# Decode attention kernel: the first weight load in two transfers, and TensorE's loop head at slot 128 of its instruction block

## The chip, the cores and the metric

One core of a Trainium2 chip runs the whole program. The metric is the device time of one execution in microseconds (us). Seven runs of the kernel before are shown, and beside them one execution that the hardware profiler recorded.

## What is computed

It is one decode step for 8 sequences: a sliding-window attention layer and then a small MLP, both behind a layer norm, in bf16. What matters of the reference:

```python
W = 2048                                   # max(256, Sk // 4), Sk = 8192
q = layernorm(x) @ wq                      # x: 8 x 512, wq: 512 x 4096, 32 heads of 128
k = repeat(k_cache[:, :, Sk - W:, :], 4)   # 8 sequences x 8 kv heads x 2048 x 128
v = repeat(v_cache[:, :, Sk - W:, :], 4)
p = softmax((q @ k^T) * 128 ** -0.5)
h = x + (p @ v).reshape(8, 4096) @ wo      # wo: 4096 x 512
y = layernorm(h)                           # then, for one token (the shifted branch is zero):
x1 = layernorm(y)
out = h + y + gelu(x1 @ w3) @ w4           # w3: 512 x 1792, w4: 1792 x 512
```

The program reads 79.18 MB from HBM: 67 MB of keys and values, 4 MB each of wq and wo, 1.8 MB each of w3 and w4.

## The kernel before, in words

**Transfers.** All large loads are issued by SyncE (SP) in `sp_prog`, on one DMA queue, in the order of the list `order`: first wq (L234, 4 MB), then keys of sequence 0 in two halves of four heads each (k, 2 MB each, L246), the first half of the last sequence's values (vl), the first quarter of wo (L252). Then, for b = 0 to 6: two key transfers of sequence b + 1 and two value transfers of sequence b, 2 MB each. At the end come the other half of the last values, the rest of wo, w3 (L258, two pieces) and w4 (L265, three pieces of 1 MB, 512 KB and 256 KB; the last has rows of 2 KB). Below, k0, k1, k2 and so on are the key transfers in order: k0 and k1 are sequence 0, k2 and k3 sequence 1. A key transfer from k2 on waits until the transposes of the keys two transfers earlier are done, since it overwrites their slot (L240: `sem_Thi`). A value transfer waits for the product that read its slot (L242). The first quarter of wo waits for the query product (L250), because it lies where wq lay. Each transfer of 128 rows is spread by rows over 16 DMA engines, eight rows for each engine.

**The query.** TensorE waits in `pe_q` for the transposed layer norm and for wq (L361), and then multiplies: 32 matmuls at L367 (`S_ps<-slots,xlnT`). The result is scaled, transposed back (L393) and put into `q_all` and `qcur`.

**The loop over sequences.** TensorE alone runs a hardware loop of 8 passes (`pe_main`, L591); the other engines' programs are unrolled. A pass (`pe_block`) transposes the keys (`pe_T`, L438, 8 steps of 16 matmuls), transposes the previous sequence's probabilities (`pe_P`, L454), sums them (`pe_LB`, L510), multiplies queries by keys (`pe_QK`, L478, 8 steps of 4) and, from the second pass on, multiplies the previous sequence's probabilities by its values (`pe_PV`, L535) and arranges the result (`pe_OP`, L554). The last two stand under an `If_ne` (L577) and are jumped over in the first pass, where there is no previous sequence. So the first pass waits for keys k0 at step 0 and for k1 at step 4, the second for k2 and k3.

**After the loop** (`pe_last` and what follows) come the last sequence's probabilities and values, the product with wo (L668, 128 matmuls), the norm's sums (L686), the product with w3 (L733, 56 matmuls) and that with w4 (L761, 56 matmuls, in three parts that each wait for their piece of w4). VectorE and ScalarE then write the two halves of the output, and SP stores it (L270).

**TensorE's instruction slots.** A matmul is two instructions, a weight load (PEld) and a matmul (PE); with fp32 operands it is two of each. A separate wait is one more. TensorE's code comes in blocks of 256 slots, and `head_slot` gives the slot of a block at which the loop's first instruction is put; what lies between is branched over. The program's own code ahead of the loop is 102 slots. A pass is 663: 384 up to and with the branch of the `If`, 276 for what it guards, 3 at the end. The code after the loop is 829 slots and follows directly.

Of the kernel before, what the change touches and what calls it, by code (L numbers as in the profile page):

```python
# [14 lines left out]
DH = 128  # L15
# [7 lines left out]
KC = D // 128  # L23
# [4 lines left out]
C = W // PP  # L28
# [8 lines left out]
def bass_sequential_preLN__sliding_block_cached__mixer_s_mlp__decode_kernel(  # L37
# [24 lines left out]
    with es:  # L62
        sb = lambda shape, dtype, name: es.enter_context(nc.sbuf_tensor(name, shape, dtype))
        ps_t = lambda shape, dtype, name: es.enter_context(nc.psum_tensor(name, shape, dtype))
        S = lambda name: es.enter_context(nc.semaphore(name))
# [3 lines left out]
        wq_sb = slots[:, NS - 2:NS, :].rearrange("p a e -> p (a e)")  # L69
# [71 lines left out]
        sem_v = [S(f"sem_v{i}") for i in range(2)]  # L141
        sem_vl = [S(f"sem_vl{i}") for i in range(2)]
        sem_x = S("sem_x")
        sem_wq = S("sem_wq")
        sem_w3 = [S(f"sem_w3_{i}") for i in range(2)]
        sem_w4 = [S(f"sem_w4_{i}") for i in range(3)]
        sem_wo = [S(f"sem_wo{i}") for i in range(3)]
# [83 lines left out]
        w4_sb = slots[:, place[("w4", 0)], 0:FC * D].rearrange("p (k n) -> p k n", k=FC)  # L231

        def sp_prog(e):
            e.dma_start(wq_sb, A_wq.rearrange("(p k) n -> p (k n)", k=KC)).then_inc(sem_wq, 16)  # L234

            for kind, t in order:
                if kind in ("k", "v", "vl"):
                    b, gq = divmod(t, 2) if kind != "vl" else (NB - 1, t)
                    if kind == "k" and b:
                        e.wait_ge(sem_Thi, NT * (t - 1))  # L240
                    if kind == "v" and b:
                        e.wait_ge(sem_PV[gq], b)  # L242
                    cache, sem, slot = {"k": (A_k_cache, sem_k, 0), "v": (A_v_cache, sem_v, 2),
                                        "vl": (A_v_cache, sem_vl, 4)}[kind]
                    src = cache[b, GL * gq:GL * (gq + 1), W0:SK, :].rearrange("g (p c) d -> p g (c d)", c=C)
                    e.dma_start(slots[:, slot + gq, :], src).then_inc(sem[gq], 16)  # L246
                    continue
                if kind == "wo":
                    if t == 0:
                        e.wait_ge(sem_peP, PEP_Q2)  # L250
                    f0, f1 = WO_CUT[t] * D, WO_CUT[t + 1] * D
                    e.dma_start(wo_sb[:, f0:f1], A_wo.rearrange("(p j) n -> p (j n)", j=NJ)[:, f0:f1]).then_inc(sem_wo[t], 16)  # L252
                    continue
                dst = slots[:, place[kind, t], :]
                if kind == "w3":
                    for i in range(2):
                        k0, k1 = i * KC // 2, (i + 1) * KC // 2
                        e.dma_start(w3_sb[:, k0:k1, :],  # L258
                                    B_w3.rearrange("(k p) f -> p k f", k=KC)[:, k0:k1, :]).then_inc(sem_w3[i], 16)
                else:  # L260
                    e.wait_ge(sem_Thi, NT * (NTILE - 1))
                    for i in range(len(W4_CUT) - 1):
                        c0, c1 = W4_CUT[i], W4_CUT[i + 1]
                        j = min(4, c1 - c0)
                        e.dma_start(w4_sb[:, c0:c1, :].rearrange("p (c j) n -> p c (j n)", j=j),  # L265
                                    B_w4[c0 * 128:c1 * 128, :].rearrange("(c p j) n -> p c (j n)", p=128, j=j)
                                    ).then_inc(sem_w4[i], 16)
            e.wait_ge(sem_dveP, DVEP_OUT_READY)
            e.wait_ge(sem_actP, ACTP_OUT_READY)
            e.dma_start(out.rearrange("b s d -> (b s) d"), out_sb[:, :]).then_inc(sem_out, 16)  # L270
            e.wait_ge(sem_out, 16)
# [86 lines left out]

        def pe_q(e):
            e.wait_ge(sem_dveP, DVEP_XLNT)  # L360
            e.wait_ge(sem_wq, 16)  # L361
            ins = None
            for k in range(2):
                for kc in range(KC):
                    for j in range(4):
                        n0 = (2 * j + k) * 512
                        ins = e.matmul(S_ps[32 * j:32 * j + B, k, :], xlnT[:, kc * B:(kc + 1) * B],  # L367
                                       wq_v[:, kc, n0:n0 + 512], start=(kc == 0), stop=(kc == KC - 1),
                                       tile_position=(0, 32 * j), skip_group_check=True)
                ins.then_inc(sem_peP, 1)  # L370
        PE.append(pe_q)

        ACTP_Q = ev_act.next()
# [187 lines left out]
        def pe_block(e, i, later=None):  # L561
            p = 2 * NT * i
            for t in range(NT):
                pe_T(e, i, t)
            pe_P(e, i, 0)
            pe_P(e, i, 1)
            pe_LB(e)
            pe_QK(e, p)
            pe_QK(e, p + 1)
            for t in range(NT, 2 * NT):  # L570
                pe_T(e, i, t)
                pe_QK(e, p + t - 2)
            pe_QK(e, p + 6)
            pe_QK(e, p + 7)
            if i == 0:
                return
            with nullcontext() if e is None else e.If_ne(later, 0):  # L577
                log.append("later")
                for gq in range(2):
                    need(e, sem_v[gq], 16 * i)  # L580
                    if e is not None:
                        pe_PV(e, 2 + gq, gq)
                pe_OP(e, i - 1)

        def pe_main(e):
            pe_block(None, 0)
            first = list(log)
            later_on = e.alloc_register("later_on")
            e.reg_mov(later_on, 0)
            log.clear()  # L590
            with nc.Fori(0, NB, engines=(mybir.EngineType.PE,), head_slot={mybir.EngineType.PE: 0}):  # L591
                pe_block(e, 1, later_on)
                e.reg_mov(later_on, 1)
            body = list(log)
            assert first == body[:body.index("later")]
            for i in range(2, NB):
                log.clear()
                pe_block(None, i)
                assert log == body, i
        PE.append(pe_main)  # L600

        for i in range(NB):
            p = 2 * NT * i
# [181 lines left out]
        with nc.Block() as block:  # L785
            block.gpsimd(pool_prog)
            block.sync(sp_prog)

            @block.tensor
            def _(e):  # L790
                for f in PE:
                    f(e)

            @block.scalar
            def _(e):
                for f in AC:
                    f(e)

            @block.vector
            def _(e):  # L800
                for f in DV:
                    f(e)
# [28 lines left out]
```

## Time and profile before

| | us |
|---|---|
| median of the 7 runs (lowest, highest) | 193.53 (193.14, 194.33) |
| the profiled execution: its time | 193.84 |
| its span, first to last instruction | 192.1 |
| TensorE (PE) busy | 145.8 |
| VectorE (DVE) busy | 85.9 |
| ScalarE (ACT) busy | 93.4 |
| wq: from its issue to its landing | 12.4 |

The profile's page gives busy times of the engines, the span cut in 40 slices with the granted TensorE clock (PEclk), the share of the DMA engines' time (DMA) and the rate (GB/s), the DMA queues, the chain of work that ended last, and the costliest groups of instructions. In the lists, "PE L668" is a TensorE matmul of line 668, "PEld" its weight load, "SPq" SyncE's sequencer. In square brackets stands how long the engine had been idle and what ended that; "issue" there means that no event in the profile ended it. Beside the lists the trace holds one record for each DMA packet (queue, start, length, bytes) and for each step of a transfer's semaphore, of which there are 16, one for each DMA engine. All times in the text are counted from the start of the span.

### The profile page before, as it was taken

Reading aid. Unit: us, or ns where it says so; the run is one execution under the profiler, and the core shown is the slowest. Engines: PE = TensorE matmul, PEld = TensorE weight load, DVE = VectorE, ACT = ScalarE, POOL = GpSimd, SP = SyncE. Lnnn points to the kernel's source line nnn. Section 1 sums busy time; section 2 is a strip of 40 time slices with the busy share of each in tenths; the row PEclk is TensorE's granted clock in tenths of the full one; section 3 lists DMA queues with packets and bytes.
Section 4 is the critical chain, followed back from the end, with each engine's and each line's share of the span. In section 5 each row is a group of like instructions: output and inputs, shape, how many; then the busy total and the mean of one; then the engine's idle time right before and its main releaser. Section 6 shows DMA issues by size and latency. Waiting matters only on the chain. (4 is left out here: it accounts for less than half of the span.)

```text
span 192.1 us, 6348 instructions
## 1 busy us (share of the span) xinstructions
PE 145.8 (76%) x2848; PEld 118.7 (62%) x2848; DVE 85.9 (45%) x183; ACT 93.4 (49%) x119; POOL 6.4 (3%) x17
## 2 busy tenths in 40 slices
PE   2038996399969964999599749997999599987654
PEld 0014964496757744876487539766976497676642
DVE  7922655155527450555174403643455245550031
ACT  3031744664476643744676436465745564552041
POOL 8400000000000000000000000000000000000000
PEclk9999999669999998799999985999799969999555
DMA  6999999999999999999999999999999999999991
GB/s 220 437 427 433 420 418 442 369 437 433 433 428 427 427 437 432 433 423 437 433 430 430 430 427 437 433 433 423 437 433 430 430 430 427 437 433 409 414 405 45
DMA packets 6329, 79.31 MB, mean 413 GB/s; under 512 B 672, under 2 KB 688, under 8 KB 1712
## 3 DMA queue, kind: packets, MB, share of 16 engines
q1 hardware_dynamic: 6304, 79.18, 97.2%
q8 instruction: 6, 0.10, 0.2%
q14 instruction: 3, 0.02, 0.0%
q10 hardware_dynamic: 16, 0.01, 0.0%
HBM read 79.18 MB, written 0.01 MB: 412 GB/s over the span
## 5 line engine op out<-in xcount | busy, mean ns | idle before, releaser
L460 ACT ACTIVATE kT_sb<-kT_ps 128x1024 bf16<-128x1024 bf16 x64 | 64.9, 1023 | 50.3 <-PE kT_ps L438 50.2
L438 PE MATMUL kT_ps<-perm_b,slots 128*128 128x128 bf16 x1024 | 76.0, 239 | 13.5 <-PEq L421 13.5
L438 PEld LDWEIGHTS kT_ps<-perm_b,slots 128*128 128x128 bf16 x1024 | 68.9, 109 | 23.7 <-issue 23.4
L464 DVE COPY kT_sb<-kT_ps 128x1024 bf16<-128x1024 bf16 x64 | 44.3, 691 | 67.6 <-PE kT_ps L438 67.6
L503 ACT ACTIVATE P_sb<-S_ps,mtile 128x1024 bf16<-128x1024 f32 x16 | 17.7, 1110 | 19.3 <-DVE mtile L498 19.3
L478 PE MATMUL S_ps<-kT_sb,qcur 128*32 128x512 bf16 x256 | 22.6, 387 | 2.9 <-PEq L421 2.9
L535 PE MATMUL misc<-slots,pT_sb 128*32 128x128 bf16 x1024 | 16.2, 219 | 1.9 <-PEq L421 1.9
L535 PEld LDWEIGHTS misc<-slots,pT_sb 128*32 128x32 bf16 x1024 | 14.7, 97 | 3.4 <-issue 3.3
L525 DVE TENSOR_TENSOR pT_sb<-kT_ps,mask 128x1024 bf16<-128x1024 bf16 x18 | 12.4, 688 | 3.6 <-PE kT_ps L454 3.5
L454 PE MATMUL kT_ps<-perm_p,P_sb 128*128 128x128 bf16 x144 | 10.9, 218 | 3.2 <-PEq L421 3.1
L478 PEld LDWEIGHTS S_ps<-kT_sb,qcur 128*32 128x32 bf16 x256 | 5.5, 93 | 10.1 <-issue 6.6
L454 PEld LDWEIGHTS kT_ps<-perm_p,P_sb 128*128 128x128 bf16 x144 | 8.4, 97 | 5.1 <-issue 4.6
L554 PE MATMUL b<-o_sum,selw 128*128 128x32 f32 x56 | 7.3, 275 | 4.3 <-PEq L421 4.3
L554 PEld LDWEIGHTS b<-o_sum,selw 128*128 128x128 f32 x56 | 6.8, 191 | 5.3 <-issue 5.3
L487 DVE TENSOR_REDUCE mtile<-S_ps 128x1 f32<-128x512 f32 x8 | 5.5, 692 | 5.0 <-PE S_ps L478 5.0
L286 DVE TENSOR_SCALAR ident_f<-iota_f 128x128 f32<-128x128 f32 x1 | 5.7, 5683 | 1.3 <-POOL iota_f L207 1.3
L344 PE MATMUL b<-ident_b,xln_b 8*128 8x8 bf16 x4 | 0.3, 175 | 7.3 <-DVE xln_b L320 7.3
L287 DVE TENSOR_SCALAR ident_b<-iota_f 128x128 bf16<-128x128 f32 x1 | 5.6, 5608 | 0.0
L544 DVE TENSOR_SCALAR o_sum<-misc,rL 128x128 f32<-128x128 f32 x8 | 2.8, 352 | 5.7 <-PE misc L535 5.7
L344 PEld LDWEIGHTS b<-ident_b,xln_b 8*128 8x128 bf16 x4 | 0.2, 115 | 8.2 <-DVE xln_b L320 8.2
L367 PE MATMUL S_ps<-slots,xlnT 128*8 128x512 bf16 x32 | 3.6, 626 | 2.0 <-DMA slots<-in_A_wq_dram 2.0
L510 PE MATMUL S_ps<-lsum,lspread 128*128 128x1 f32 x36 | 5.0, 243 | 0.0
(91 smaller groups left out, 66.2 us busy)
## 6 DMA issues: line engine op xcount, KB each, us to landing
slots<-in_A_k_cache_dram SPq DMA_DIRECT2D x16, 2048.0 KB, 12.8
slots<-in_A_v_cache_dram SPq DMA_DIRECT2D x16, 2048.0 KB, 17.0
slots<-in_A_wq_dram SPq DMA_DIRECT2D x1, 4096.0 KB, 12.4
slots<-in_A_wo_dram SPq DMA_DIRECT2D x2, 1024.0 KB, 21.7
slots<-in_A_wo_dram SPq DMA_DIRECT2D x1, 2048.0 KB, 26.3
slots<-in_B_w_dram SPq DMA_DIRECT2D x2, 896.0 KB, 31.3
slots<-in_B_w_dram SPq DMA_DIRECT2D x1, 1024.0 KB, 28.7
slots<-in_B_w_dram SPq DMA_DIRECT2D x1, 512.0 KB, 28.6
```

The source lines that it names most:

```text
L286: e.tensor_single_scalar(ident_f[:], iota_f[:], 0.0, ALU.is_equal)
L287: ins = e.tensor_single_scalar(ident_b[:], iota_f[:], 0.0, ALU.is_equal)
L438: ins = e.matmul(kT_ps[t % 2][:, c * 128:(c + 1) * 128], src[:, c * 128:(c + 1) * 128], perm_b[:, :], is_transpose=True)
L454: ins = e.matmul(kT_ps[half][:, c * 128:(c + 1) * 128], P_sb[:, k * 128:(k + 1) * 128], perm_p[:, :], is_transpose=True)
L460: e.activation(kT_sb[:, i % NKT, 0:W // 2], kT_ps[i % 2][:, 0:W // 2], ACT.Copy).then_inc(sem_Elo, 1)
L464: e.tensor_copy(kT_sb[:, i % NKT, W // 2:W], kT_ps[i % 2][:, W // 2:W]).then_inc(sem_Ehi, 1)
L478: ins = e.matmul(S_ps[32 * gl:32 * (gl + 1), 0, :], qcur[:, GL * gq + gl, o:o + 32], kv[:, gl, :, :], start=(t == 0), stop=(t == 2 * NT - ...
L487: ins = e.tensor_reduce(mtile[:, 1, 0:1], S_ps[:, 0, :], AX.X, ALU.max)
L503: e.activation(P_sb[:, half * W // 2:(half + 1) * W // 2].rearrange("r (k g) -> r k g", g=GL), bass.AP(tensor=S_ps[:, :, :].tensor, offset ...
L525: e.tensor_tensor(bass.AP(tensor=pT_sb[:, :, :, :].tensor, offset=h0 * NT * 48, ap=[[CT * NT * 48, 128], [48, CT // 2 * NT], [32, 2], [1, ...
L535: ins = e.matmul(pv_ps[32 * q:32 * (q + 1), :], pT_sb[:, c, q, 16 * gq:16 * gq + 32], slots[:, slot, k * DH:(k + 1) * DH], start=(gq == 0 ...
L554: ins = e.matmul(op_ps(b), selw[:, q, :], o_sum[:, NJ * q:NJ * (q + 1)], start=(q == 0), stop=(q == 3))
```

## The change

Two edits. The load of wq becomes two transfers with a semaphore each: columns 0 to 1023 of each row of 16,384 (rows of 2 KB, 256 KB in all), and the other 15,360 columns (rows of 30 KB, 3.75 MB). TensorE waits for both before its first product. And the head of TensorE's loop is put at slot 128 of its block where it was at slot 0. The order of the instructions on each engine is otherwise the same.

```diff
-        sem_wq = S("sem_wq")
+        sem_wq = [S(f"sem_wq{i}") for i in range(2)]
...
         def sp_prog(e):
-            e.dma_start(wq_sb, A_wq.rearrange("(p k) n -> p (k n)", k=KC)).then_inc(sem_wq, 16)
+            wq_rows = A_wq.rearrange("(p k) n -> p (k n)", k=KC)
+            for i, (n0, n1) in enumerate(((0, 1024), (1024, 2 * C * DH))):
+                e.dma_start(wq_sb[:, n0:n1], wq_rows[:, n0:n1]).then_inc(sem_wq[i], 16)
...
         def pe_q(e):
             e.wait_ge(sem_dveP, DVEP_XLNT)
-            e.wait_ge(sem_wq, 16)
+            for sem in sem_wq:
+                e.wait_ge(sem, 16)
...
-            with nc.Fori(0, NB, engines=(mybir.EngineType.PE,), head_slot={mybir.EngineType.PE: 0}):
+            with nc.Fori(0, NB, engines=(mybir.EngineType.PE,), head_slot={mybir.EngineType.PE: 128}):
```

## The prediction

> **What bounds the kernel now.** I read the page first: the slices, the queues and the chain.
>
> ```profile
> DMA  6999999999999999999999999999999999999991
> GB/s 220 437 427 433 420 418 442 369 437 433 433 428 427 427 437 432 433 423 437 433 430 430 430 427 437 433 433 423 437 433 430 430 430 427 437 433 409 414 405 45
> ...
> q1 hardware_dynamic: 6304, 79.18, 97.2%
> q8 instruction: 6, 0.10, 0.2%
> ...
> DMA slots<-in_B_w_dram 15%; PE kT_ps L438 3%; SPq L265 1%; PE b L761 1%; DVEq L785 0%; DVE xln_b L772 0%
> ```
>
> The DMA engines are full from the second slice to the last but one, and the chain ends on the landing of w4. So the end is one stream of 79.18 MB: at the 431 GB/s of its undisturbed part (118 us of the third view) it needs 184 us, and what is lost is at three places: the start (220 GB/s), the slice from 33.6 us (369) and the last four. Next I read the start, the hole and the middle as stretches (us; PE, PEld, DVE, ACT, POOL busy; clock; DMA share; GB/s):
>
> ```profile
> 0.00:2.00 2.00, 0.00 (x0) 0.00 (x0) 0.67 (x2) 0.64 (x1) 1.44 (x13) 1.00 0.65 167
> 2.00:4.00 2.00, 1.00 (x2) 0.13 (x2) 2.00 (x2) 0.84 (x2) 2.00 (x4) 1.00 0.71 263
> 34.00:38.00 4.00, 1.50 (x15) 1.53 (x16) 0.18 (x2) 2.75 (x5) 0.00 (x0) 0.60 0.99 369
> 55.00:173.00 118.00, 98.40 (x1948) 81.85 (x1948) 54.28 (x110) 64.50 (x81) 0.00 (x0) 0.93 1.01 431
> ```
>
> The hole at 34 to 38 us is explained by the order of time around the first pass:
>
> ```profile
> 0.73 0.41 SPq L234 DMA_DIRECT2D slots<-in_A_wq_dram  x1
> 1.20 1.29 SPq L246 DMA_DIRECT2D slots<-in_A_k_cache_dram  x2
> 13.23 3.58 PE L367 MATMUL S_ps<-slots,xlnT 128*8 128x512 bf16 x32 [1.97 <-DMA slots<-in_A_wq_dram]
> 18.51 5.17 PE L438 MATMUL kT_ps<-perm_b,slots 128*128 128x128 bf16 x64
> 36.50 6.17 PE L438 MATMUL kT_ps<-perm_b,slots 128*128 128x128 bf16 x64 [4.06 <-PEq L421]
> ```
>
> k3 can be issued only when the first pass has transposed k1: SP issues it at 31.16. By the packet records five engines start k3 at 34.01 to 34.22 with packets of 0.98 to 1.76 us where 0.61 is usual, and two stand idle for 0.7 and 1.0 us: the queue had run dry, and refills slowly. So until k3 the time goes from wq's landing (13.09) over the query and the first pass to k3's issue; after that the stream never runs dry. An earlier wq is an earlier end, for most engines. Engines that had been held up before the hole fill it with their backlog: k2's semaphore steps are at 34.3 to 35.0 on 14 engines and at 36.22 and 36.36 on two, k3's at 39.6 to 41.3.
>
> **The head of wq: the gain.** In the packet records the sixteen first packets (32 KB) start at 1.78 to 2.65 us and take 1.36 to 2.26 us; later ones take 1.21. Measured by when each engine ends its first packet, it is behind a full-rate stream begun at 1.78 by 0.64 to 1.34 us, 0.96 on average: 0.25 is the later start, 0.71 the slow packet. How a first packet of 2 KB goes no row shows. The nearest is the load of x at 0.74 us: eight 1 KB packets, seven of 44 ns and one of 259, so 0.03 us too many on average. 2 KB rows in full stream are the last piece of w4: 84 ns each, against 76 ns for 2 KB at the rate of the 32 KB packets; eight of them cost 0.07 us more. With these, 0.25 + 0.03 + 0.07 = 0.35 us are lost instead of 0.96: **0.61 us gained**. The upper bound is all 0.71 of the slow packets. The lower: the second piece is issued 0.47 us after the first (the spacing of wq and k0 above) and pays the slow packet all the same. Then it is 0.47 later with 256 KB less to carry (0.61 us at 431 GB/s) and the 0.07 for rows: 0.07 gained. With the extra of the hole (1.0 in place of 0.71) it is 0.2 lost. Range: 0.2 lost to 0.7 gained. I take 0.61, by the row of x, since it is the only start with small rows.
>
> SP's extra issue puts k0, k1, vl back by 0.47 us; they lie behind 9.7 us of wq's data and cost nothing; if the cover were gone it would be 0.47. The second wait in `pe_q` ends with the later piece, and behind it stands only the query product. The transposed norm it also needs is done at 11.46, so wq can be 1.6 us earlier before that is late; k0 shifts with the stream. Few packets are smaller, so the rate after the head stays.
>
> The 256 KB piece has an exact match: the last piece of w4. These two weight loads follow the landings of its two last pieces:
>
> ```profile
> 188.62 0.31 PEld L761 LDWEIGHTS b<-slots,gT 128*8 128x8 bf16 x16 [0.39 <-DMA slots<-in_B_w_dram]
> 189.26 0.10 PEld L761 LDWEIGHTS b<-slots,gT 128*8 128x8 bf16 x8 [0.33 <-DMA slots<-in_B_w_dram]
> ```
>
> They are 0.64 us apart, 256 KB at nearly full rate. [...]
>
> **The loop head.** The body's block borders are now at slots 256 and 512 and, after the loop, at slots 105, 361 and 617 of that code; with the head at 128 they lie at body slots 128, 384 and 640 and at 233, 489 and 745 of the tail. Each border shows in the trace: a 16 KB instruction packet on q8 at 21.59, 29.62, 36.40, 176.41, 182.34 and 187.04, each 2 to 4 us after TensorE passes into a new block, for the block after that. So a block that is run through in under some 5 us stalls, and one does, 18 matmuls into L668, which is tail slot 361:
>
> ```profile
> 176.64 0.61 PE L668 MATMUL S_ps<-opl,slots 128*128 128x8 bf16 x18 [0.22 <-ACT opl L559]
> 178.67 3.10 PE L668 MATMUL S_ps<-opl,slots 128*128 128x8 bf16 x110 [1.42 <-issue]
> ```
>
> Packet 176.41 to 177.35, TensorE on at 178.67: 5.7 us after the border at 105 (about 173.0), 1.3 after the packet. *Tail, after:* the border at 489 is 80 matmuls into L668; its block is asked for at slot 233 (about 174.0) and is there at 179.7. The last 32 matmuls need the last piece of wo (lands 180.63), so this stall lies beside that. L668 ends 0.2 us earlier at most, and L761 waits for w4 0.7 us anyway: 0. *First pass, after:* two costs. Slot 128 is reached 62 matmuls into L438, at about 23.3; if the head's block is entered only at 18.4, the next is there at 22.47 + 1.3 = 23.8: up to 0.5 us, on the path to k3. If the code ahead of the loop is short enough to share the head's block, that next block is there already: 0. Nothing in the trace shows which; I take 0, and 0.5 for the range. And the `If` at body slot 383 now jumps to 660 over a whole block, which nobody has asked for: asked for at 32.4, there at 38.1 to 38.7, where k2 lands at 36.36. TensorE's second pass starts up to 2.2 us later. That is covered: k5, issued at 50.15, would come at 52.3, and with k3's 2.85 us to the first packet at 55.2. The first engine is through with k4 at 54.2, the last at 55.9, so only engines 1.7 us ahead wait. Its pass ends 0.9 us before k4 lands, so the delay is gone in two passes.
>
> [...]
>
> **Sum.** 193.84 - 0.61 = 193.23 for the profiled execution, which is 0.31 above the median: 192.9.
>
> **Rivals.**
> *A, the head's gain is lost* (second piece starts as slowly as the first did, or 0.5 us at slot 128 eats it): 193.5, 193.0 to 193.9. For it: packets are slow after a dry queue whatever their size (1.0 us extra at 34 us). Against: x's small rows were not.
> *B, slower: instruction fetch in the first pass.* 0.5 us at slot 128 with no gain at the head; and if the jumped-to block and the one after it are fetched one after the other, TensorE is 4 us late where the last engine bears 2.6 (k5 needed at 55.6 - 2.85 = 52.75, issued at 50.15): 1.4 more. 194.0 to 195.4, say 194.4. It decides from 2.6 us of delay. Against: six packets in the whole run say that blocks, once loaded, stay.
> *C, the slot does nothing* (blocks lie elsewhere than I count): the head alone, 192.9 too.
>
> **Numbers.** Forecast with C 0.47, A 0.30, B 0.23. Under 0.3% (0.58 us, about what a measurement of this kernel can tell from no change) lies 192.95 to 194.11: faster 0.47, same 0.30, slower 0.23. The range runs from 192.3 (all of the slow packets and 0.5 us of luck in which engine an instruction packet hits: the last engine lands 0.45 after the next) to 194.4 (B).
>
> **What would show it.** Right: wq lands at about 12.5, first long packets without the extra 0.7, k3 issued at about 30.6, w4 landing 0.6 earlier. The slot: a stall inside the first 64 matmuls of L438, a start of the second pass at 38 instead of 36.5, the gap in L668 moved to its 80th matmul. Wrong: wq landing at 13 again, more than eight q8 packets, a hole in the GB/s row after 50 us.

## The result, and the profile after

The changed kernel is **slower: 194.84 us median of 13 runs (194.09 to 196.58)** beside 193.46 (193.01 to 194.66, 34 runs) for the kernel before on the same chip. The ratio is 1.0076, with a 95% interval of 1.0055 to 1.0097, so about 1.4 us were lost. 192.9 was predicted, and the range ended at 194.4. The profiled execution took 195.85 us (span 194.1), 1.0 above its own median, so it shows the losses large; a second profile of the same kernel further down took 194.97.

Line numbers have moved: L367 is now L370, L438 is L441, L668 is L671, L246 is L248, L761 is L764. The slices of the page first:

```profile
PEclk9999999759999996699999988999799999999555
...
GB/s 258 405 422 432 426 424 437 429 429 432 432 317 414 426 432 427 432 432 429 432 432 432 429 432 432 432 432 432 432 432 432 432 432 432 432 429 411 412 335 14
...
q8 instruction: 7, 0.11, 0.2%
...
DMA slots<-in_B_w_dram 15%; PE kT_ps L441 2%; SPq L267 1%; PE b L764 1%; DVEq L788 0%; DVE xln_b L775 0%
```

Three things are to be read in the row of GB/s. The head, which was to gain 0.6 us, gained next to nothing: the first two slices carry 258 + 405 = 663 in place of 220 + 437 = 657, and with slices of 4.85 us in place of 4.80 that is 3217 KB by 9.70 us in place of 3155 KB by 9.60, some 20 KB or **0.05 us** more than at an equal time. The hole in the eighth slice (369) is gone (429). And a new hole has come in the twelfth slice, 53 to 58 us (317). There is one instruction packet more on q8, and the chain of waits still ends on w4.

The same as stretches (us; PE, PEld, DVE, ACT, POOL busy; clock; DMA share; GB/s):

```profile
34.00:38.00 4.00, 0.00 (x0) 0.00 (x0) 0.00 (x0) 2.07 (x4) 0.00 (x0) 0.79 1.03 434
38.00:55.00 17.00, 15.90 (x308) 13.33 (x308) 8.46 (x17) 8.35 (x9) 0.00 (x0) 0.85 0.99 413
55.00:173.00 118.00, 96.91 (x1924) 80.03 (x1924) 53.97 (x110) 65.74 (x83) 0.00 (x0) 0.94 1.01 428
```

From 34 to 38 us TensorE does nothing at all, where it had done 15 matmuls before, and the DMA engines are full (434 GB/s in place of 369). TensorE in order of time, the start of the first, the second and the third pass:

```profile
12.98 3.28 PE L370 MATMUL S_ps<-slots,xlnT 128*8 128x512 bf16 x32 [1.73 <-DMA slots<-in_A_wq_dram]
17.85 1.95 PE L441 MATMUL kT_ps<-perm_b,slots 128*128 128x128 bf16 x32
20.02 1.78 PE L441 MATMUL kT_ps<-perm_b,slots 128*128 128x128 bf16 x29 [0.23 <-PEq L424]
23.00 0.33 PE L441 MATMUL kT_ps<-perm_b,slots 128*128 128x128 bf16 x3 [1.20 <-issue]
38.39 5.98 PE L441 MATMUL kT_ps<-perm_b,slots 128*128 128x128 bf16 x64 [6.34 <-PEq L424]
56.48 3.98 PE L441 MATMUL kT_ps<-perm_b,slots 128*128 128x128 bf16 x64
```

After 32 + 29 = 61 matmuls TensorE stops for 1.20 us and nothing in the profile ends the wait ("issue"): this is the block border at body slot 128, and the instruction packet ahead of it runs from 20.80 to 21.73. The second pass starts at 38.39, though its keys k2 landed at 36.16. I read this as the jump over a whole block (the instruction packet ahead of it runs from 35.43 to 36.40); a sequencer wait (PEq) is shown since the pass begins with a wait that had long been met. The 64 transposes of the second pass then take 5.98 us where those of the third take 3.98: in the trace's clock records the granted clock is 0.5 from 36.30 to 43.12 us, after TensorE has stood idle, and 1.0 again from there. (Before it was 0.5 from 34.83 to 41.66, and the same 64 took 6.17.) k4 waits for these transposes, and k5 comes 7.45 us behind k4, so this slow stretch is a part of k5's lateness in either kernel. SP's transfers of keys:

```profile
23.36 7.95 SPq L248 DMA_DIRECT2D slots<-in_A_k_cache_dram  x2
44.39 7.98 SPq L248 DMA_DIRECT2D slots<-in_A_k_cache_dram  x2
```

These are k2 with k3 and k4 with k5; an issue takes 0.53, so k3 goes out at 30.77 (31.16 before) and k5 at 51.84 (50.15 before). The end of the tail, where the change was to cost nothing, and did not by itself:

```profile
180.21 1.87 PE L671 MATMUL S_ps<-opl,slots 128*128 128x8 bf16 x64 [1.98 <-DMA slots<-in_A_wo_dram]
```

The stall inside the product with wo is gone (1.42 us before); TensorE waits there for the DMA alone. The two weight loads behind the last pieces of w4:

```profile
190.62 0.31 PEld L764 LDWEIGHTS b<-slots,gT 128*8 128x8 bf16 x16 [0.37 <-DMA slots<-in_B_w_dram]
191.26 0.10 PEld L764 LDWEIGHTS b<-slots,gT 128*8 128x8 bf16 x8 [0.32 <-DMA slots<-in_B_w_dram]
```

They are 0.64 us apart as before, and both 2.00 us later. So the chain ends as it did, on the landing of w4, and what has to be explained is that landing: 191.22 for the last engine in place of 189.21. Of these 2.01 us, 0.77 are in the mean over the engines and 1.22 in how far the last one is behind it.

In the table, all from the semaphore steps, "mean" is over the 16 DMA engines, and an undisturbed 2 MB transfer puts the mean 4.86 later than the one ahead. Hole 1 is what the step from k2 to k3 has beyond that, hole 2 what the two steps from the last value transfer ahead of k4 to k5 have beyond 9.72. "Lead" is the time from k5's issue to the mean end of k4, had it run undisturbed. "Last" is how far the last engine is behind the mean at w4's landing. "Full matmul rate by" is where the trace's clock records begin, with full clock; there the matmuls' durations fall too (experiment 4). The kernels below the first two are explained with their experiments.

| profiled execution (its time) | full matmul rate by | k3 issued | hole 1 | 2nd pass | k5 issued | lead | hole 2 | w4 mean | last |
|---|---|---|---|---|---|---|---|---|---|
| before (193.84) | 21.2 | 31.16 | 0.67 | 36.50 | 50.15 | 4.79 | 0.06 | 188.03 | +1.19 |
| after (195.85) | 15.8 | 30.77 | 0.11 | 38.39 | 51.84 | 2.50 | 1.46 | 188.80 | +2.41 |
| after again (194.97) | 22.2 | 31.45 | 0.72 | 39.63 | 52.42 | 2.63 | 0.18 | 188.23 | +2.00 |
| slot 128 alone (194.69) | 17.4 | 31.41 | 0.80 | 38.58 | 51.23 | 3.85 | 0.07 | 188.24 | +1.73 |
| changed, old tail (196.09) | 21.3 | 31.68 | 0.75 | 39.27 | 53.28 | 1.77 | 0.94 | 189.21 | +2.21 |
| changed, dummies (196.38) | 21.7 | 31.83 | 0.72 | 39.99 | 53.87 | 1.19 | 1.25 | 189.68 | +1.98 |
| split alone (193.19) | 17.0 | 29.80 | 0.00 | 36.61 | 49.85 | 4.44 | 0.08 | 187.38 | +1.19 |
| split, early full rate (193.13) | 13.4 | 29.51 | 0.11 | 36.06 | 49.45 | 4.83 | 0.08 | 187.37 | +1.12 |
| split in halves (193.55) | 20.8 | 30.86 | 0.62 | 36.22 | 49.83 | 4.94 | 0.08 | 187.86 | +1.06 |
| split, held by 0 (193.69) | 22.2 | 31.42 | 0.34 | 36.17 | 48.99 | 5.57 | 0.08 | 187.65 | +1.40 |
| split, held by 4 (193.25) | 17.4 | 29.88 | 0.11 | 38.65 | 51.26 | 3.07 | 0.12 | 187.45 | +1.17 |
| split, held by 4, again (194.63) | 15.7 | 29.48 | 0.00 | 38.25 | 51.71 | 2.64 | 0.88 | 188.45 | +1.55 |
| split, held by 5 (197.53) | 21.9 | 31.32 | 0.65 | 42.64 | 55.50 | -0.70 | 3.14 | 191.42 | +1.47 |

### The profile page after: what moved, and what is told of

Read it like the earlier page. It is cut to its first block, busy times and chain, and to the rows that moved or that the text cites. A ratio compares the mean times of both kernels' runs of the same rounds, so it can differ in the third digit from the quotient of the medians.

```text
span 194.1 us, 6349 instructions
## 1 busy us (share of the span) xinstructions
PE 142.3 (73%) x2848; PEld 114.7 (59%) x2848; DVE 85.8 (44%) x183; ACT 92.8 (48%) x119; POOL 6.4 (3%) x17
## 5 line engine op out<-in xcount | busy, mean ns | idle before, releaser
L441 PE MATMUL kT_ps<-perm_b,slots 128*128 128x128 bf16 x1024 | 72.1, 232 | 17.0 <-PEq L424 15.6
L441 PEld LDWEIGHTS kT_ps<-perm_b,slots 128*128 128x128 bf16 x1024 | 64.7, 105 | 27.5 <-issue 27.3
L557 PE MATMUL b<-o_sum,selw 128*128 128x32 f32 x56 | 7.8, 285 | 4.3 <-PEq L424 4.3
L671 PE MATMUL S_ps<-opl,slots 128*128 128x8 bf16 x128 | 3.8, 168 | 2.8 <-DMA slots<-in_A_wo_dram 2.6
L671 PEld LDWEIGHTS S_ps<-opl,slots 128*128 128x128 bf16 x128 | 3.6, 102 | 3.0 <-DMA slots<-in_A_wo_dram 2.7
```

The source lines that it names most:

```text
L441: ins = e.matmul(kT_ps[t % 2][:, c * 128:(c + 1) * 128], src[:, c * 128:(c + 1) * 128], perm_b[:, :], is_transpose=True)
L557: ins = e.matmul(op_ps(b), selw[:, q, :], o_sum[:, NJ * q:NJ * (q + 1)], start=(q == 0), stop=(q == 3))
L671: ins = e.matmul(hT_ps[:, k * B:(k + 1) * B], wo_at(h)[:, k * 128:(k + 1) * 128], opl[:, h, :], start=False, stop=(h == NJ - 1), skip_grou ...
```

## The experiments

**The theory after the result:** the head gains little; the second pass, some 2 us late, issues k5 so late that the DMA queue runs dry, and this costs more than the head gains. **The rivals:** the instruction packets and their places cost (which engine one hits, which border stalls, in the loop or in the tail); or the split of wq costs.

### 1. One half of the change at a time

Split alone: the head of the loop back at slot 0.

```diff
-            with nc.Fori(0, NB, engines=(mybir.EngineType.PE,), head_slot={mybir.EngineType.PE: 128}):
+            with nc.Fori(0, NB, engines=(mybir.EngineType.PE,), head_slot={mybir.EngineType.PE: 0}):
```

> The two transfers of wq alone, loop head at slot 0 as before. Theory (the time comes from the loop head: the If of the first pass jumps over a whole block of code, the second pass starts 2 us late, the fifth key transfer k5 is issued 1.7 us late, and the DMA queue runs dry at 53 to 57 us): no hole after 50 us, second pass at about 36.3, time 193.0 to 193.6, ratio 0.997 to 1.001. Rival 1 (the small piece and the 30 KB rows cost the time): 194.5 or more, as in the changed kernel. Rival 2 (no hole matters, only the engine that TensorE's instruction packets hit after 175 us): the borders after the loop are those of before, so 193.2 to 193.6 too.

Slot alone: the kernel before, wq in one transfer, with the head at 128.

```diff
-            with nc.Fori(0, NB, engines=(mybir.EngineType.PE,), head_slot={mybir.EngineType.PE: 0}):
+            with nc.Fori(0, NB, engines=(mybir.EngineType.PE,), head_slot={mybir.EngineType.PE: 128}):
```

> The loop head at slot 128 alone, wq in one transfer. Theory: second pass at about 38.5, k5 issued at about 52, hole at 53 to 57 us, 194.5 to 195.2, ratio 1.005 to 1.010. Rival 1 (the split costs it): 193.3 to 193.7. Rival 2 (instruction packets at the end): 194 to 195, with the last step of w4 more than 1 us behind the last but one, and no matter whether there is a hole.

Measured: the split alone 193.18 us, ratio 0.997 (0.9948 to 0.9992); the slot alone 195.22 us, ratio 1.0071 (1.0041 to 1.01). **The slot is the whole loss, and the split is at most a small gain.** The page of the split alone has neither hole:

```profile
GB/s 262 411 418 435 414 423 430 431 435 438 435 430 418 425 435 433 431 435 438 431 421 425 435 435 431 435 438 421 431 425 435 435 431 435 435 421 416 409 407 45
```

The list of TensorE of the slot alone has the same two marks as the changed kernel, the stall after 61 matmuls and the late second pass:

```profile
23.64 0.33 PE L438 MATMUL kT_ps<-perm_b,slots 128*128 128x128 bf16 x3 [1.20 <-issue]
38.58 5.17 PE L438 MATMUL kT_ps<-perm_b,slots 128*128 128x128 bf16 x64 [5.89 <-PEq L421]
```

In this execution the stall put k3 at 31.41, and hole 1 is there (0.80) while hole 2 is not (0.07): k5 went out at 51.23, into a stream that hole 1 had made later, so its lead was 3.85. A fourth early instruction packet, at 41.52, seems to hit the engine that is last already: the last landing of the next values is 5.90 behind the last one of k3, 1.04 more than 4.86. So this run is 1.5 us slower than the split alone (193.19) with no hole 2 at all: 0.86 of the w4 landing are in the mean, nearly all of it hole 1, and 0.54 in the last engine.

### 2. Other places of the borders

Head at slot 64: the borders lie at body slots 192, 448 and at another place of the tail.

```diff
-... head_slot={mybir.EngineType.PE: 128}):
+... head_slot={mybir.EngineType.PE: 64}):
```

> The two transfers of wq, and the loop head at slot 64: block borders at body slots 192 and 448, so the first pass's jump from 383 to 660 goes into the next block and over none; the borders after the loop are at 41, 297, 553 and 809. Theory: that next block was asked for some 6 us ahead, second pass at 36.2 to 36.5, no hole after 50 us, 193.0 to 193.6. Rival 1 (the split): 194.5 or more. Rival 2 (packets at the end): four packets after 172 us, on other engines: anything from 193.2 to 195, without a hole.

Measured: 196.23 us, ratio 1.01 (1.0066 to 1.0134). **No theory had this.** The loop is as with slot 0 (second pass at 36.57, k5 at 50.17, no hole 2), and the stream ends earlier than before (188.64), but TensorE now ends last. Its list for the tail:

```profile
172.44 2.07 PE L538 MATMUL misc<-slots,pT_sb 128*32 128x128 bf16 x127
178.00 0.23 PE L538 MATMUL misc<-slots,pT_sb 128*32 128x128 bf16 x1 [3.49 <-issue]
184.89 0.54 PE L671 MATMUL S_ps<-opl,slots 128*128 128x8 bf16 x14 [0.56 <-issue]
190.47 1.67 PE L764 MATMUL b<-slots,gT 128*8 128x128 bf16 x56
```

A block border now lies on the last matmul of the last sequence's product with its values, and there TensorE stands for 3.49 us; in the kernels with slot 0 or 128 that product runs through (x128 in one line). The last product starts at 190.47 without a wait in brackets: w4 had been there since 188.64, so this kernel's end is the instruction fetch of the tail. The two stops are also a measure of a block: by the count of instructions they come after 298 and 554 slots of the code after the loop, 256 apart, and the trace's instruction packets on q8 have 16,384 bytes each.

The changed kernel's loop with the tail of the kernel before (its first instruction aligned to slot 151, where it lay):

```diff
+            e.addr_align(256, offset=151, max_nops=0)
```

> The changed kernel, with the code after the loop put back to the slot of its block at which it stood before (151): its block borders are again at 105, 361 and 617; the loop head stays at 128. Theory (the jump over a block makes k5 late and opens the hole at 53 to 57 us): the hole stays, 194.3 to 195.3. Rival (only the borders after the loop, so the instruction packets after 175 us, cost the time): 193.2 to 193.7 with the hole still there.

Measured: 194.23 us, ratio 1.0045 (1.0019 to 1.0071). It is still slower than the kernel before, so the tail's borders alone do not explain the loss; the point estimate lies below the changed kernel's 1.0076, but the intervals overlap.

The reverse, the loop at slot 0 with the changed kernel's tail (aligned to slot 23):

```diff
+            e.addr_align(256, offset=23, max_nops=0)
```

> The two transfers of wq with the head at slot 0, and the code after the loop put to slot 23 of its block, as the changed kernel has it (borders at 233, 489 and 745). Theory: no hole, and the stall of 1.4 us inside the product with wo goes, which only waits for w4 in any case: 193.0 to 193.5, as with the head at slot 0 alone. Rival (borders after the loop): 194.3 or more.

Measured: 195.51 us, ratio 1.0108 (1.0079 to 1.0137), for a reason that has no part in the changed kernel. One line of TensorE's list:

```profile
176.23 1.14 PE L538 MATMUL misc<-slots,pT_sb 128*32 128x128 bf16 x34 [2.76 <-issue]
```

In the changed kernel the block with this border had been fetched in the first pass already (the packet at 40.97; there is no other until 177.70); here it has not been, and is asked for only at 173.86. So the two halves of a border's cost are not additive: here the tail stalls 2.76 us on a block that the loop's first pass had not loaded, and in the changed kernel, where by the packets it had, the same product runs through in 2.12 us. A second stop in this tail, of 1.31 us, comes 81 matmuls into the product with wo, after 488 slots, and the one above after 232: 256 apart again.

### 3. Cover for the late k5

The other half of the last values (vl, 2 MB) moved from the end of the list to between k4 and k5, so that the queue has 4.86 us more work when k5 comes.

```diff
-            order += [("k", 2 * b + 2), ("k", 2 * b + 3), ("v", 2 * b), ("v", 2 * b + 1)]
-        order += [("vl", 1), ("wo", 1), ("wo", 2), ("w3", 0), ("w4", 0)]
+            order += [("k", 2 * b + 2)] + [("vl", 1)] * (b == 1) + [("k", 2 * b + 3), ("v", 2 * b), ("v", 2 * b + 1)]
+        order += [("wo", 1), ("wo", 2), ("w3", 0), ("w4", 0)]
```

> The changed kernel, with the second half of the last values (2 MB, its place is free all the time) issued between k4 and k5 and no longer at the end: the queue has 4.9 us more in hand when k5 is late. TensorE still jumps over the block. Theory: second pass still at about 38.4, k5 still issued at about 52, but no hole: 1.4 us of it come back, 193.2 to 193.9. Rival 1 (the split): 194.5 or more. Rival 2 (packets at the end): 194.3 or more, with the last step of w4 still more than 1 us behind the last but one.

Measured: 197.7 us, ratio 1.0187 (1.0144 to 1.023). The cover works: the second pass starts at 39.41 and k5 goes out only at 53.46, and the step to k5 is 4.91. The time does not show it, because the last keys now land 4.9 us later and the tail becomes TensorE's: the DMA is done at 189.88, and the output is issued at 195.03. A remedy in the wrong place, and no verdict on the theory but for the missing hole.

### 4. The matmul rate at the start

Between the profiles the first pass differs by more than a microsecond. In the profile before a matmul of the transposes takes 311 ns at first and 219 from some moment on; from one matmul to the next it is 106 ns and then 56 (311 and 107 are also what it takes at 37 to 41 us, where the clock records show 0.5). That moment lay at 15.7 to 22.2 us in the executions with nothing added for it, and differs between executions of one kernel (15.8 and 22.2 in the two of the changed kernel). PEclk on the page is 0.9 or more in all these slices and does not show it: the trace has no clock record ahead of that moment, and its first one, with full clock, begins there. Where it comes late, the 64 transposes take 5.2 to 5.6 us in place of some 4.1, and k3 is issued at 30.9 us or later; then there is a hole 1. What sets that moment no run shows; the first three clock records of the profile after, with full, half and full clock, last 20.48, 6.83 and 30.72 us.

If the loss were lost time of the first pass, an early full rate would repay it. That more products ahead of the query bring it on was a guess of mine. First with 20 more products of one row each ahead of the query, on the split with slot 0 and on the changed kernel (their result is overwritten):

```diff
-            for k in range(2):
-                e.matmul(S_ps[:, k, :], zrow_b[0:1, :], x_sb[0:1, :], start=True, stop=True)
+            for k in range(2 + 16):
+                e.matmul(S_ps[:, k % 2, :], zrow_b[0:1, :], x_sb[0:1, :], start=True, stop=True)
...
+            for k in range(4):
+                e.matmul(S_ps[:, k % 2, :], zrow_b[0:1, :], x_sb[0:1, :], start=True, stop=True)
```

> The two transfers of wq with the head at slot 0, and 20 more matmuls of 512 columns on TensorE while it waits for wq (zeros into a place that the query product overwrites). It tests what sets the hole at 34 us and the two groups of times before (193.1 and 194.0): the clock granted to TensorE rises to full at 16 to 21 us, by chance, and the transposes of the first pass take 5.2 or 4.1 us with it. Theory: full clock before 13 us, query product in some 2 us, k3 issued at 28 to 29 in every run, never a hole, and times in one group: 192.9 to 193.2. Rival (the clock does nothing, the two groups come from which engine an instruction packet hits): no difference from the head at slot 0 alone, 193.2 to 193.4, both groups still there.

> The changed kernel with the same 20 matmuls. The jump over the block stays, and its fetch still takes some 5.5 us, but the first pass ends 1.5 us earlier. Theory: second pass at about 36.5, k5 issued at about 50, little or no hole after 50 us, 193.2 to 193.9. Rival (borders after the loop): still 194.5 or more. Rival (the split): the same.

Measured: 193.29 us, ratio 0.999 (0.9964 to 1.0016), and 195.75 us, ratio 1.0106 (1.0073 to 1.0139). The dummies failed: in the first of the two kernels eighteen products of one row ran on end for 7.8 us, from 2.33 on, at 427 ns each throughout, and the full rate came at 16.0 and at 21.7, within the range of the kernels without them. The second is no repair, and shows hole 2 once more (1.25).

Then with 30 products of full size (128x128 by 128 columns), from 9.2 us on, on the split with slot 0:

```diff
+            for k in range(14):
+                e.matmul(S_ps[:, 1, 0:128], perm_b[:, :], ident_b[:, :], start=True, stop=True)
...
+            for k in range(16):
+                e.matmul(S_ps[:, 1, 0:128], perm_b[:, :], ident_b[:, :], start=True, stop=True)
```

> The two transfers of wq, head at slot 0, and 30 matmuls of 128 x 128 with real numbers (identity by permutation) from 9.1 us on, before and after the transposes of the norm. The first try, with a weight of one row, left the clock at half until 16 us (427 ns for 512 columns throughout) and so did not test what it was made for. Theory (the clock of the first pass decides whether k3 is late): full clock from 13 to 16 us on in every run, the 64 transposes of the first pass in 4.1 us and never 5.2, k3 issued at 29.8 or before, no hole, 192.8 to 193.2 and no group at 194. Rival (the clock does not decide): 193.0 to 193.4 with some runs above 193.9.

Measured: 193.22 us, ratio 0.9986 (0.9961 to 1.0011). This time the rate is there. TensorE's list, to be set beside 3.58 and 5.17 us for the same two products before:

```profile
13.24 1.93 PE L384 MATMUL S_ps<-slots,xlnT 128*8 128x512 bf16 x32 [0.17 <-DMA slots<-in_A_wq_dram]
18.10 3.93 PE L455 MATMUL kT_ps<-perm_b,slots 128*128 128x128 bf16 x64 [1.43 <-PEq L438]
```

Nearly 3 us of TensorE's time are gone from the start, and the kernel is no faster than the split alone: once hole 1 is closed, k3 earlier still is worth nothing. Ten of its twelve runs lie within 193.09 and 193.37, but ten of the twelve of the split alone lie as close together (193.01 to 193.29), so the times do not show that the early rate keeps hole 1 away.

### 5. Do the small rows matter?

wq in two equal halves (rows of 16 KB), loop at slot 0:

```diff
-            for i, (n0, n1) in enumerate(((0, 1024), (1024, 2 * C * DH))):
+            for i, (n0, n1) in enumerate(((0, C * DH), (C * DH, 2 * C * DH))):
```

> wq in two equal halves (rows of 16 KB each), head at slot 0: two transfers, but no small rows. If small first rows shorten the start, wq lands 0.2 us later than with them (13.1 for 12.9) and the time is 193.3 to 193.6; if the second transfer or chance makes the difference, wq lands at 12.9 again and the time is 193.1 to 193.3.

Measured: 193.16 us, ratio 0.9984 (0.9955 to 1.0013); wq lands at 12.64 mean and 12.82 last, as early as with 2 KB rows (12.62 to 12.72 mean in the other split kernels; 12.76 and 12.67 in the two profiles with wq in one piece). **Small rows are not what the head needs,** and neither form gains more than 0.15 us on the mean.

### 6. Lateness without any block effect

Split with slot 0, and every pass of TensorE waits for a semaphore that GpSimd raises: at once for the first pass, after a number of memsets behind the first pass' products for the second and later ones. The blocks lie as in the split alone, up to that one wait.

```diff
+            e.memset(idle[:, NDELAY, 0:2], 0.0).then_inc(sem_pass, 1)
+            e.wait_ge(sem_QK, 8)
+            for j in range(NDELAY):
+                e.memset(idle[:, j, :], 0.0)
+            for i in range(1, NB):
+                e.memset(idle[:, NDELAY, 2 * i:2 * i + 2], 0.0).then_inc(sem_pass, 1)
...
+            need(e, sem_pass, i + 1)
```

With four memsets:

> The two transfers of wq with the loop head at slot 0, so that no jump misses, and one more wait at the head of each pass, on a semaphore that GpSimd raises; for the second pass it does so only after four memsets of 128 x 2048 (some 7 us) behind the first pass's last product. So the second pass starts at 38 to 39.5 us for a reason that has nothing to do with code blocks. Theory (a late second pass makes k5 late and dries the queue): k5 issued at 52 to 53, a hole of 1 to 2 us at 53 to 58, 194.2 to 195.5. Rival (the hole comes with the blocks themselves, by their packets): no hole, 193.0 to 193.6.

With none, as a control:

> Control for the kernel with the late second pass: wq in two pieces, head at slot 0, the per-pass wait of TensorE on GpSimd's semaphore is there, but GpSimd raises it without the four 128x2048 memsets, so that the second pass starts when k2 lands (about 36.5 us). If lateness of the second pass is what costs, this runs like the split with slot 0: ratio to before 0.996 to 0.999, about 193.2 us, second pass at 36.1 to 36.8 us, k5 issued at 49 to 50.2. If the added wait itself costs, it runs like the kernel with the delay: 1.004 to 1.007, about 194.6.

A second profile with four:

> A second look at the kernel with four memsets, whose only profile was its fastest run (193.25 where its median is 194.72). Lateness theory: in an ordinary run of 194.4 to 195.2 the second pass starts at 39 to 39.6 us, k5 is issued after 51.8 and the step from k4's mean landing to k5's is 0.5 to 1.5 us over 4.86. Rival (something else in this kernel costs): the step stays at 4.9 to 5.0 in a run of 194.4 or more.

With five, of 128x2240:

> Dose: the second pass held by five memsets of 128x2240 (some 2.0 us each by the 1.82 us of 128x2048), so until about 41.0 us where four held it until 38.3 to 38.7; k5 is issued at about 53.9 to 54.1 in place of 51.3 to 51.7. No code block is touched. If the loss comes from k5 issued after the engines run dry: the second look at four memsets had k5 at 51.71 and a step from k4's to k5's mean landing of 5.72 for 4.87, so here 2.2 to 2.4 more, a step of 7.9 to 8.2, and a time of 196.3 to 197.0 (ratio 1.014 to 1.019); the hold with no delay ran at 0.999. If the loss of the delay does not follow its length: 194.4 to 195.2.

Measured: four memsets 194.72 us, ratio 1.0056 (1.0027 to 1.0085); none 193.28 us, ratio 0.9991 (0.9959 to 1.0023); five 196.49 us, ratio 1.0153 (1.0118 to 1.0188). The wait itself costs nothing, four memsets cost 0.65% more than none (0.2 to 1.1 by the two intervals), or **about 1.3 us, with three early instruction packets as before and no border moved**. The first profile of the four was the fastest of its twelve runs (193.25) and has hardly a hole 2 (0.12); the second took 194.63, and its page and its second pass are:

```profile
GB/s 260 408 418 435 432 408 442 421 425 428 428 381 413 435 432 430 435 432 435 428 428 432 421 435 435 432 435 411 432 435 432 432 432 428 432 428 415 409 391 32
```

```profile
38.25 5.98 PE L450 MATMUL kT_ps<-perm_b,slots 128*128 128x128 bf16 x64 [7.50 <-PEq L433]
```

The hole stands in the twelfth slice (381), where the changed kernel has its own (317); TensorE's second pass starts at 38.25 as there (38.39). The same pass in the first profile, without the hole:

```profile
38.65 5.13 PE L450 MATMUL kT_ps<-perm_b,slots 128*128 128x128 bf16 x64 [7.50 <-PEq L433]
```

It starts 0.40 later and yet sends k5 0.46 earlier: the clock records show 0.5 until 41.28 us there and until 43.01 in the second profile, and so the transposes take 5.13 and 5.98. So k5's issue depends on the start of the second pass and on how long the half clock lasts. The memsets run in both profiles, so they are not the loss themselves. With five memsets, page and list are:

```profile
GB/s 256 408 422 435 435 429 415 385 429 432 335 278 410 432 432 432 430 429 429 429 429 432 429 435 435 429 432 405 422 429 429 432 429 429 432 432 429 406 398 37
```

```profile
42.64 5.38 PE L451 MATMUL kT_ps<-perm_b,slots 128*128 128x128 bf16 x64 [10.04 <-PEq L434]
```

The hole fills two slices (335 and 278). The pass came 1.6 us later than expected (42.64 for 41.0), and the dose shows: k5 goes out 3.79 later than in the second profile of four, and hole 2 is 3.14 in place of 0.88. The step from k4 to k5 alone is 6.59, not 7.9 to 8.2, since 1.4 us of the hole fall on k4 itself, which takes the packets' slowness too; hole 2 has both in it, and with one normal step it makes 8.0.

### 7. The changed kernel again

> The changed kernel again, for a second trace and more times. Theory: 194.3 to 195.2, second pass at 38 to 39.5, with a hole after 53 us; if the clock rises late, also one at 34 us. Rival (the borders after the loop): holes or not, the last step of w4 is over 1 us behind the last but one.

Measured: 195.28 us, ratio 1.0081 (1.0052 to 1.011); the result stands. In this execution the full rate came late and hole 1 was there (0.72), and hole 2 is only 0.18; in the first profile it was the other way round (0.11 and 1.46). The sum of both holes is 0.90 and 1.57, against 0.73 in the kernel before and 0.08 in the split alone. In this execution, 1.8 us slower than the split alone, hole 1 and the last engine (2.00 behind) make up most of the loss, and hole 2 next to none.

## Why the prediction was wrong, point by point

**The jump over a whole block: the time was right, its price was wrong.** This is the step that failed. I put the second pass at 38.1 to 38.7 (measured 38.39 to 39.99 in six profiles with slot 128, 36.1 to 36.6 otherwise) and k5's issue at 52.3 (51.84), and then wrote "That is covered", with "only engines 1.7 us ahead wait" and "k5 needed at 55.6 - 2.85 = 52.75". Rival B had the same bound ("2.6 us of delay"); k5 at 51.84, 1.69 later than before, was enough. The table says where the cover really ends: with a lead of 3.07 us or more no profile without extra cover has a hole 2 over 0.12, and with 2.64 or less each of them has one, from 0.18 to 3.14. So the 2.85 us that I read off k3 was about the right lead, but it has to be there for the mean engine, and I took the end of the *last* one. (How large the hole is does not follow closely: with leads of 2.64, 2.63, 2.50, 1.77 and 1.19 it is 0.88, 0.18, 1.46, 0.94 and 1.25. Why it was so small in the one profile stays open.) Two more things went against it. Where the queue is nearly dry, packets become slow, and the last engine loses too: in the profile after, thirty packets begun from 53.46 to 56.52 us took 0.67 to 1.97 us where 0.61 is usual, and the last engine's step from k4 (55.55) to k5 (61.96) is 6.41. And the stream itself had become earlier by closing hole 1 (its mean 0.60 ahead at the last values before k4: 49.48 in place of 50.08), so that k5 was needed 0.6 sooner: **what hole 1 gave back went into hole 2.** The reverse holds too: with hole 1 at 0.72 and 0.80, hole 2 is 0.18 and 0.07 in the two other profiles of slot 128 without a further edit. The delay alone, made by other means, costs 1.3 us (experiment 6); how much of the loss it is in an ordinary run of the changed kernel is not shown. I had also taken the slow second pass (6.17 us for 64 transposes, at half clock) as it stood in the row, and nothing in my sum asked how long the half clock would last.

**The stall at body slot 128: taken as 0, measured 1.20.** I had left open which block holds the head and bounded it by 0.5 from a slow first pass. With the full matmul rate from 16 to 18 us TensorE is at the border sooner, and then the stall is 1.20; with a late rate it is 0.20, 0.31 and 0.47 in three profiles and lost among slow matmuls in the sixth. In the profile after k3 was still 0.39 earlier than before; in the slot alone, where the stall is 1.20 as well, k3 went out at 31.41 and hole 1 is 0.80.

**The head of wq: 0.61 predicted, 0.05 to 0.14 measured** on the mean landing (0.05 by the slices, 12.62 for 12.76 by the steps; 0.25 by the last step). The row of x misled: eight 1 KB packets with one slow one said that small rows start quickly. In the profile after, 2 KB packets took up to 0.61 us in place of 0.084, on average 0.24 too long in all for an engine, and the first 30 KB packet of each engine took 1.18 to 1.67 in place of 1.14. The second piece pays the start once more, which was my own lower bound (0.07). The split alone is still ahead by 0.3% (0.0008 to 0.0052 of the time), with the five kernels that have the split and slot 0, the tail unmoved and no pass held back, between 0.997 and 0.9991; four of the five intervals include 1. What that gain comes from is open, since wq's landing moved by 0.14 us at most.

**The instruction packet on the last engine: in the range as luck, and it came each time.** At w4's landing the last engine is 1.7 to 2.4 us behind the mean in every profile of a kernel with slot 128, and 1.0 to 1.55 in all others. I had counted eight packets at most; after the first pass there is a fourth one at 41 to 43 us, which in four of the six profiles seems to fall on the engine that is last already, by the last steps around it. 16 KB take it 0.9 us, and with the next packet slow it is some 1.0 to 1.25 behind. In the profile after it was another packet (177.70). At the landing of w4 the last engine's lag is 1.22, 0.81 and 0.54 more than in the profile before, for the profile after, the changed kernel again and the slot alone; the mean is 0.77, 0.20 and 0.21 later. This is the part of the loss that the late second pass does not explain: 1.7 to 2.1 us between the split alone and the changed kernel, less 1.3 to 1.4 for the delay, leaves 0.3 to 0.8. No run has the packet without the delay, so that share is argued from the landings, not shown, and in the two profiles with a small hole 2 it is the larger one.

**Right:** SP's extra issue and the second wait cost nothing; the 256 KB piece, with others queued behind it, cost no more than its bytes; the gap in the product with wo went without a later stall; hole 2 "after 50 us" was named as the sign of being wrong; rival B named the mechanism, instruction fetch in the first pass, and its span of 194.0 to 195.4 holds the median of 194.84. The place was named and the chance put at 0.23, since I weighed six packets in the whole run as a sign that blocks stay; that they stay says nothing of the first time through.

**Best version:** the split with the loop at slot 0, 193.18 us, and level with it within the intervals the halves and the early full rate.

## What to carry to other kernels

When a producer of transfer requests is made later, compare its issue time with the moment at which the *average* queue will be empty, less the time from issue to first packet as measured on the same queue (2.85 us here; 3.07 were enough in these profiles, and 2.64 were not), and do it on the schedule as it will be after the other edits, since a stream made earlier at one place needs its next request earlier too. A move of code by half a block is no small edit: here a border reached 4.0 to 6.4 us after TensorE had passed the one before it (4.0 in the first pass of the changed kernel, 4.2 in the tail before, 6.4 with the tail at slot 23), or a first jump over a block, showed as microseconds of "issue" or as a late pass, and a block that the loop has loaded can be what the tail lives on (without it the tail at slot 23 stood 2.76 us). A gain at the start of a stream is worth only what the next bound lets through; read it off the landings before pricing the end.

## What the runs showed of the hardware that was not expected

- A DMA queue does not simply pause when it is short of work: thirty packets that otherwise take 0.61 us took 0.67 to 1.97 us within some 3 us around the moment, and a hole in the mean of 1.46 us came from a request that was 0.35 us later than the lead of 2.85.
- A border reached for the first time held TensorE for 3.49 us (head at slot 64), 2.76 (tail at slot 23) and 1.20 (the changed kernel) in different places; the packet itself takes 0.88 to 1.06 us of an engine in the two profiles before and after.
- The matmul rate nearly doubles (one transpose each 56 ns in place of 106) at a moment that differs from run to run by 6.5 us, unseen in PEclk on the page. With thirty products of full size it came at 13.4 us, in one profile; eighteen products of one row, 7.8 us on end, did not bring it.
- Within a stop of TensorE between two passes (6.34 us) its clock fell to half for 6.83 us, and the next pass paid for it: 64 transposes in 5.98 us in place of 3.98.
- Cutting the first large load in two, at 2 KB or at 16 KB, moved its mean landing by 0.15 us at most.
